# Part B of a gated attention kernel: batched token attention around two memory-row chains

## The chip, the cores and the metric

The kernel runs on one core of a Trainium2 chip. The metric is the device time of one launch in microseconds; TensorE is the matmul engine, DVE, ACT and POOL are the vector, scalar and GpSimd engines, SP only issues transfers. A granted clock of 1.00 is TensorE at full speed.

## What is computed

A token sequence x of 2048 rows by 576 goes through two attentions, and a gate mixes them; the outputs are the result and the gradients of eleven inputs for a given grad_out. Cut to what matters:

```python
# A: multi-query attention, 32 heads of 18, one key and value head
q = x @ wq; k = x @ wk; v = x @ wv
a = softmax(q k^T / sqrt(18)) v @ wo
# B: 64 segments of 32 tokens; 8 memory rows go from one to the next; 32 heads of 128
mem = mem0
for s in range(64):
    h = concat([mem, x[32*s : 32*s+32]])            # 40 rows
    q, k, v = h @ Wq, h @ Wk, h @ Wv
    mask = (row < 8) | (row >= col)                 # memory rows see all
    p = softmax(where(mask, q k^T / sqrt(128), -1e9))
    o = (p v) @ Wo
    mem = o[:8]; outs.append(o[8:])
g = sigmoid(sum(x * gate_w))
out = g * a + (1 - g) * b                           # and the gradients of all of it
```

Only the memory rows go from one segment to the next, in the forward pass from first to last and in the backward pass from last to first. The queries, keys and values of the tokens need no memory row. A token's attention needs the eight memory rows of its own segment.

## The kernel before

Part A (its functions are not in the diff but for the order of constants ahead of them) runs first and takes about a third of the span. Part B follows in stages, each with its own pools of on-chip memory, so a stage begins when the one before has given up its pools.

`b_forward` loops over 64 segments. A segment takes the 40 rows, padded to 64, as `hTs` (columns are tokens, then memory rows). For q, k and v, four banks `pbank` each take two groups of 64 output rows, in pieces of 102 or 103 columns; a piece is five contraction tiles by two groups of matmuls. Then come transposes into `ptrh`, scores `pkq` with a mask matmul, Exp, row sums and a reciprocal on DVE, and p·v in two layouts (`oT`, `o2`). 192 matmuls of eight columns (`psmall`) make the next eight memory rows, which ACT copies into the next `hTs`; this closes the loop from segment to segment. q, k, v, p and o are stored for the way back (`st_q2` to `st_oT`).

`make_transposed_weights`, `gate_combine_pass` and the load of the transposed weights follow. `b_backward` loops over the segments in reverse with the same 64-row layout: the gradient `gTs` times Wo (`pbank<-WoT,gTs`), products for dS, dq, dk and dv in two layouts, and 480 matmuls of 40 columns (`pdh`) for the gradient of the rows. `b_epilogue` computes the weight gradients from the stored rows (`epib`, `epiwo`), and `dx_combine` adds up the gradient of x.

Helpers: `mm` issues a matmul, `tr` a transpose (also on TensorE), `evac` copies a bank out on DVE and ACT in turn. POOL and SP issue the transfers; POOL also fills buffers and does some products of part A. In names, `bufs=2` means that a tile has two buffers.

Of the kernel before, what the change touches and what calls it, by code (L numbers as in the profile page):

```python
# [20 lines left out]
LP = 64  # L21
# [8 lines left out]
MNK_LIMIT = 960000  # L30
BIG_LIMIT = None


def plane(h):
    return h // 16


def ucol(h):
    return (h % 16) // 4, (h % 4) * 128


def pieces(N, M, K, limit="default"):
    lim = MNK_LIMIT if limit == "default" else limit
    if lim is None or M * N * K <= lim:
        return [(0, N)]
    maxn = max(1, lim // (M * K))
    n = (N + maxn - 1) // maxn
    base = N // n
    rem = N % n
    out = []  # L50
    lo = 0
    for i in range(n):
        sz = base + (1 if i < rem else 0)
        out.append((lo, lo + sz))
        lo += sz
    return out


def pieces_b(N, M, K):
    return pieces(N, M, K, limit=BIG_LIMIT)  # L60


class Kern:

    def __init__(self, tc, T, A_x, A_wq, A_wk, A_wv, A_wo, B_mem0, B_Wq, B_Wk, B_Wv, B_Wo,
                 gate_w, grad_out, outs, extras=None):
# [6 lines left out]
        assert T % P == 0  # L73
# [10 lines left out]
        self.extras = extras or {}  # L84
# [20 lines left out]
    def setup_consts(self, pool):  # L105
# [7 lines left out]
        self.onesB = pool.tile([P, 64], BF16, name="onesB")  # L113
        nc.gpsimd.memset(self.onesB[:], 1.0)
        self.negonesB = pool.tile([P, 64], BF16, name="negonesB")
        nc.gpsimd.memset(self.negonesB[:], -1.0)
        mb = pool.tile([P, 64], BF16, name="maskbias")
        nc.gpsimd.memset(mb[:], 0.0)
        nc.gpsimd.affine_select(out=mb[0:64], in_=mb[0:64], compare_op=ALU.is_ge, fill=NEGB,
                                base=0, pattern=[[1, 64]], channel_multiplier=-1)  # L120
        nc.gpsimd.affine_select(out=mb[0:64], in_=mb[0:64], compare_op=ALU.is_ge, fill=0.0,
                                base=31, pattern=[[0, 64]], channel_multiplier=-1)
        nc.gpsimd.affine_select(out=mb[0:64], in_=mb[0:64], compare_op=ALU.is_ge, fill=NEGB,
                                base=39, pattern=[[0, 64]], channel_multiplier=-1)
        nc.gpsimd.affine_select(out=mb[0:32], in_=mb[0:32], compare_op=ALU.is_ge, fill=NEGB,
                                base=39, pattern=[[-1, 64]], channel_multiplier=0)
        nc.gpsimd.affine_select(out=mb[32:64], in_=mb[32:64], compare_op=ALU.is_ge, fill=0.0,
                                base=39, pattern=[[-1, 64]], channel_multiplier=0)
        nc.gpsimd.affine_select(out=mb[32:40], in_=mb[32:40], compare_op=ALU.is_ge, fill=NEGB,
                                base=39, pattern=[[-1, 64]], channel_multiplier=0)  # L130
        self.maskbias = mb

    def setup_dram(self, dram):
        T, NSEG, NM = self.T, self.NSEG, self.NM
        NMP = ((NM + P - 1) // P) * P
        self.xT_dram = dram.tile([NKT, P, T], BF16, name="xT_dram")
        self.st_q2 = dram.tile([NSEG, P, 2048], BF16, name="st_q2")
        self.st_k2 = dram.tile([NSEG, P, 2048], BF16, name="st_k2")
        self.st_vT = dram.tile([NSEG, P, 2048], BF16, name="st_vT")
        self.st_pnT = dram.tile([NSEG, P, 2048], BF16, name="st_pnT")  # L140
        self.st_oT = dram.tile([NSEG, P, 2048], BF16, name="st_oT")
        self.st_WT = dram.tile([3, HB, P, D], BF16, name="st_WT")
        self.st_WoT = dram.tile([NKT, P, J], BF16, name="st_WoT")
        self.ox_dram = dram.tile([T, J], BF16, name="ox_dram")
        self.om_dram = dram.tile([NMP, J], BF16, name="om_dram")
        self.dbT_dram = dram.tile([NKT, P, T], BF16, name="dbT_dram")
        self.dqx_dram = dram.tile([T, J], BF16, name="dqx_dram")
        self.dqm_dram = dram.tile([NMP, J], BF16, name="dqm_dram")
        self.dkx_dram = dram.tile([T, J], BF16, name="dkx_dram")
        self.dkm_dram = dram.tile([NMP, J], BF16, name="dkm_dram")  # L150
        self.dvx_dram = dram.tile([T, J], BF16, name="dvx_dram")
        self.dvm_dram = dram.tile([NMP, J], BF16, name="dvm_dram")
        self.dxB_dram = dram.tile([T, D], BF16, name="dxB_dram")
        self.dm_dram = dram.tile([NMP, D], BF16, name="dm_dram")
        self.db_dram = dram.tile([T, D], BF16, name="db_dram")
        self.da_dram = dram.tile([T, D], BF16, name="da_dram")
        self.b_dram = dram.tile([T, D], F32, name="b_dram")
        self.a_dram = dram.tile([T, D], BF16, name="a_dram")
        self.mtok_dram = dram.tile([NMP, D], BF16, name="mtok_dram")

    def build_xT(self, work, psum, keep):
        nc = self.nc
        T, NTT = self.T, self.NTT
        xT = keep.tile([P, NKT, T], BF16, name="xT")
        for tt in range(NTT):
            xt = work.tile([P, D], BF16, name="xtok", bufs=2)
            nc.sync.dma_start(xt[:], self.A_x[tt * P:(tt + 1) * P, :])
            tp = psum.tile([P, 6, P], BF16, name="trx", bufs=2)
            for kt in range(4):
                nc.tensor.transpose(tp[:, kt, :], xt[:, kt * P:(kt + 1) * P], self.identB[:])  # L170
            nc.tensor.transpose(tp[0:64, 4, :], xt[:, 512:576], self.identB[:])
            nc.tensor.transpose(tp[64:128, 4, :], xt[:, 512:576], self.identB[:], tile_position=(0, 64))
            self.evac(xT[:, :, tt * P:(tt + 1) * P], tp[:, 0:5, :])
        for kt in range(NKT):
            nc.sync.dma_start(self.xT_dram[kt], xT[:, kt, :])
        return xT

    def load_B_weights_fwd(self, pool, wo_pool=None):
        nc = self.nc
        wo_pool = wo_pool or pool  # L180
# [4 lines left out]
        self.Wv5 = pool.tile([P, J], BF16, name="Wv5")  # L185
        for W4, Wd in ((self.Wq4, self.B_Wq), (self.Wk4, self.B_Wk), (self.Wv4, self.B_Wv)):
            for kt in range(4):
                eng = nc.sync if kt % 2 == 0 else nc.gpsimd
                eng.dma_start(W4[:, kt, :], Wd[kt * P:(kt + 1) * P, :])
        nc.sync.dma_start(self.Wqk5[0:64, :], self.B_Wq[512:576, :])  # L190
        nc.gpsimd.dma_start(self.Wqk5[64:128, :], self.B_Wk[512:576, :])
        nc.sync.dma_start(self.Wv5[0:64, :], self.B_Wv[512:576, :])
        nc.gpsimd.memset(self.Wv5[64:128, :], 0.0)
        self.WoN = wo_pool.tile([P, HB, D], BF16, name="WoN")
# [959 lines left out]
def build_full(tc, A_x, A_wq, A_wk, A_wv, A_wo, B_mem0, B_Wq, B_Wk, B_Wv, B_Wo, gate_w, grad_out, outs_raw,  # L1154
# [9 lines left out]
    with SB("const") as cpool, tc.tile_pool(name="dram", bufs=1, space=bass.MemoryType.DRAM) as dram:  # L1164
# [24 lines left out]
        with SB("xsp") as xsp:  # L1189
            k.dx_combine(xsp)  # L1190
# [76 lines left out]
```

## Time and profile before

| | |
|---|---|
| median of 3 runs | 14871.25 us (14867.74 to 14881.40) |
| profiled execution | 14893.78 us, span 14892.1 us, mean granted clock 0.596 |
| TensorE busy | 13545.5 us, 91% |
| DVE, ACT, POOL busy | 38%, 26%, 9% |
| part A | 0 to 5140 us |
| B forward | 5201 to 10423 us |
| transposes, gate pass, loads | 10423 to 10931 us |
| B backward | 10931 to 13977 us |
| weight gradients, dx | 13977 to 14892 us |

The profiled execution is one of several; its time is 0.15% above the median. Busy times are of one engine each and lie side by side, so they don't add up to the span. An instruction's row gives the tile that it writes, then `<-` and what it reads, then the partitions by elements of its operands.

### The profile page before, as it was taken

Reading aid. Unit: us, or ns where it says so; the run is one execution under the profiler, and the core shown is the slowest. Engines: PE = TensorE matmul, PEld = TensorE weight load, DVE = VectorE, ACT = ScalarE, POOL = GpSimd, SP = SyncE. Lnnn points to the kernel's source line nnn. Section 1 sums busy time; section 2 is a strip of 40 time slices with the busy share of each in tenths; the row PEclk is TensorE's granted clock in tenths of the full one; section 3 lists DMA queues with packets and bytes.
Section 4 is the critical chain, followed back from the end, with each engine's and each line's share of the span. In section 5 each row is a group of like instructions: output and inputs, shape, how many; then the busy total and the mean of one; then the engine's idle time right before and its main releaser. Section 6 shows DMA issues by size and latency. Waiting matters only on the chain. (4 is left out here: it accounts for less than half of the span.)

```text
span 14892.1 us, 355211 instructions
## 1 busy us (share of the span) xinstructions
PE 13545.5 (91%) x163790; PEld 7557.7 (51%) x163790; DVE 5585.9 (38%) x6393; ACT 3815.3 (26%) x4970; POOL 1269.2 (9%) x2548
## 2 busy tenths in 40 slices
PE   8999999999999899999999999999679999999896
PEld 2121121211212266666666666666568888888632
DVE  5555555555555323323232333323223333333201
ACT  3444444444444211111111111111112222222100
POOL 1000000000000000000000000000111111111225
PEclk6555555555555655555555555555667777777899
DMA  1000000000000211111111111111542222222334
GB/s 53 1 3 3 1 3 3 1 3 1 3 1 1 74 38 39 37 40 39 37 39 37 40 37 39 37 40 39 173 133 80 80 77 80 82 82 80 122 130 112
DMA packets 432921, 715.36 MB, mean 48 GB/s; under 512 B 212145, under 2 KB 288834, under 8 KB 428546
## 3 DMA queue, kind: packets, MB, share of 16 engines
q1 hardware_dynamic: 326466, 394.62, 8.6%
q0 software_dynamic: 103648, 296.68, 6.0%
q8 instruction: 1280, 20.97, 0.6%
q14 instruction: 215, 1.76, 0.0%
q10 hardware_dynamic: 1312, 1.33, 0.0%
HBM read 363.20 MB, written 329.19 MB: 46 GB/s over the span
## 5 line engine op out<-in xcount | busy, mean ns | idle before, releaser
L98 PEld LDWEIGHTS <-hTs 128*64 128x64 bf16 (+1 forms) x38400 | 1854.9, 150 | 948.0 <-DVE hTs L250 61.2
L1046 DVE TENSOR_TENSOR a_U<-a_w,a_E 128x1024 bf16<-128x1024 f32 x1024 | 1251.7, 1224 | 1131.8 <-ACT a_E L1044 1088.6
L973 DVE TENSOR_TENSOR a_U<-a_w,a_E 128x1024 bf16<-128x1024 f32 x1024 | 1253.1, 1224 | 963.1 <-ACT a_E L971 962.8
L1044 ACT ACTIVATE a_E<-a_w 128x1024 bf16<-128x1024 f32 x1024 | 1049.1, 1025 | 1375.6 <-PE a_w L98 1374.4
L971 ACT ACTIVATE a_E<-a_w 128x1024 bf16<-128x1024 f32 x1024 | 1048.8, 1025 | 1179.5 <-PE a_w L98 1179.5
L309 DVE RECIPROCAL rden<-pbank 64x512 f32<-64x512 f32 x256 | 840.5, 3322 | 482.3 <-PE pbank L98 482.3
L98 PE MATMUL pbank<-Wv,hTs 128*64 128x103 bf16 (+3 forms) x12800 | 912.4, 290 | 0.0
L98 PE MATMUL a_w<-a_kaug,a_qaug 19*128 19x512 bf16 x2048 | 901.7, 600 | 4.8 <-ACT a_E L1044 4.1
L98 PE MATMUL a_w<-a_vaugT,a_doaT 19*128 19x512 bf16 x2048 | 836.0, 620 | 21.8 <-DVE a_U L1046 15.9
L98 PE MATMUL pbank<-Wq,hTs 128*64 128x103 bf16 (+1 forms) x10240 | 710.5, 290 | 81.8 <-DVE hTs L250 60.9
L98 PE MATMUL pbank<-Wqk,hTs 64*64 64x102 bf16 (+1 forms) x5120 | 753.2, 291 | 0.0
L98 PE MATMUL pbank<-WoT,gTs 128*64 128x103 bf16 (+3 forms) x12800 | 672.7, 234 | 55.9 <-DMA WoT<-st_WoT 52.3
L98 PE MATMUL pbank<-Wk,hTs 128*64 128x103 bf16 (+1 forms) x10240 | 711.1, 290 | 0.0
L98 PE MATMUL a_acc<-a_E,a_dog 128*32 128x512 bf16 x2048 | 625.0, 600 | 71.8 <-ACT a_E L1044 0.2
L98 PE MATMUL a_w<-a_doT,a_vaugT 19*128 19x512 bf16 x2048 | 670.8, 623 | 5.2 <-ACT a_E L971 4.1
L98 PE MATMUL a_w<-a_qaug,a_kaug 19*128 19x512 bf16 x2048 | 658.0, 599 | 3.6 <-ACT a_doT L95 3.0
L98 PE MATMUL a_acc<-a_U,a_ku 128*32 128x512 bf16 x2048 | 625.3, 607 | 0.2
L98 PE MATMUL a_acc<-a_U,a_qtok 128*32 128x512 bf16 x2048 | 623.3, 606 | 0.6 <-DVE a_U L1046 0.6
L98 PEld LDWEIGHTS <-gTs 128*64 128x64 bf16 (+1 forms) x12800 | 476.0, 117 | 247.8 <-issue 57.8
L98 PE MATMUL pkq<-qT,kT 128*64 128x64 bf16 x2048 | 534.3, 261 | 0.0
L98 PE MATMUL pkq<-maskbias,identB 64*64 64x64 bf16 x2048 | 530.3, 259 | 0.0
L98 PE MATMUL epib<-dcol,h_x 128*128 128x512 bf16 (+1 forms) x1920 | 458.3, 382 | 59.7 <-DMA dcol<-dqx_dram 25.3
(393 smaller groups left out, 16761.8 us busy)
## 6 DMA issues: line engine op xcount, KB each, us to landing
st_q<-q SPq DMA_DIRECT2D x64, 512.0 KB
st_k<-k POOLq DMA_DIRECT2D x64, 512.0 KB, 2.9
st_vT<-vT SPq DMA_DIRECT2D x64, 512.0 KB
st_pnT<-pnT SPq DMA_DIRECT2D x64, 512.0 KB
st_oT<-oT POOLq DMA_DIRECT2D x64, 512.0 KB, 4.1
bq<-st_q SPq DMA_DIRECT2D x64, 512.0 KB
bvT<-st_vT SPq DMA_DIRECT2D x64, 512.0 KB
bk<-st_k POOLq DMA_DIRECT2D x64, 512.0 KB, 4.6
```

What stands on the lines that cost most here:

```text
L98: return self.nc.tensor.matmul(out, lhsT, rhs, start=start, stop=stop, tile_position=tp, skip_group_check=True)
L309: nc.vector.reciprocal(rden[rows, :], den[rows, :])
L971: nc.scalar.activation(ex[:], s[:], ACT.Exp, scale=SCALEA)
L973: nc.vector.tensor_tensor(out=u[:], in0=d[:], in1=ex[:], op=ALU.mult)
L1044: nc.scalar.activation(ex[:], s[:], ACT.Exp, scale=SCALEA)
L1046: nc.vector.tensor_tensor(out=u[:], in0=d[:], in1=ex[:], op=ALU.mult)
```

## The change

Part B is rewritten in stages. `b_project` makes q, k and v of all tokens in 16 tiles of 128, in both layouts (`XT` by token, `XE` by head column), and stores them, with k and v once more by segment (`XS`). `b_transpose_weights` follows in the same pools. `b_chain_fwd` goes over the 64 segments with the eight memory rows alone: 32 columns of `c_mT`, of which eight are this segment's rows, stand as weight in each of four groups of 32 columns of the array, and a group computes an eighth of the heads over 512 columns. A quad of four such matmuls goes to one bank. The scores of the memory rows with tokens and memory are one bank (`c_S`), with the mask added by a matmul; division by the row sums comes after p·v. The output (`c_pw`) leaves partial sums in four row groups, and five fp32 matmuls with a selector (`selF`) add these and give the next columns of `c_mT`. `b_x_attention` then takes 16 tiles by two halves of heads: forward attention of 128 tokens at once with a block mask, the gate and its gradient, and the token part of the backward pass. `b_chain_bwd` carries the gradient of the memory rows backwards, in the same way, `b_x_gradients` finishes dk, dv and dx of the tokens, `b_mem_rows` brings the chain's gradients into rows, and `b_weight_gradients` sums over 16 + 4 row tiles with 512-column matmuls. The gate pass, `b_epilogue` and `dx_combine` are gone as stages of their own.

`setup_consts` makes five masks and selectors on POOL where it made one.

The diff, cut to the parts that the prediction speaks of:

```diff
-    def b_forward(self, wpool, sp, psum, wo_pool=None):
...
-        for s in range(NSEG):
-            nc.sync.dma_start(hTs[:, :, 0:SEG], self.xT_dram[:, :, s * SEG:(s + 1) * SEG].rearrange("k p t -> p k t"))
...
-                    for (lo, hi) in pcs:
-        for kt in range(NKT):
...
-                            for (c, base) in ((u, 0), (u + 4, 64)):
-                                cols = slice(c * 512 + lo, c * 512 + hi)
-                                self.mm(pb[base:base + 64, lo:hi], lhsT=hTs[lrows, kt, :], rhs=wap[rows, cols],
-                                        start=(kt == 0), stop=(kt == NKT - 1), tp=(lrows.start, base))
...
-                    nc.vector.reciprocal(rden[rows, :], den[rows, :])
...
-    def b_backward(self, wpool, sp, psum):
...
+        def keep_block(t, n, lo, hi):
+            nc.gpsimd.affine_select(out=t, in_=t, compare_op=ALU.is_ge, fill=NEGB, base=-lo,
...
+        mc = pool.tile([P, 512], BF16, name="maskC")
+        mx = pool.tile([P, 4, P], BF16, name="maskX")
+        mm_ = pool.tile([P, 4, P], BF16, name="maskM")
...
+    def b_project(self, keep, sp, psum):
...
+        for tt in range(NTT):
+            tok = slice(tt * P, (tt + 1) * P)
+            for w in "kvq":
+                tk = sp.tile([P, J], BF16, name="p_tok", bufs=2)
+                te = sp.tile([P, 2, 4, 4, P], BF16, name="p_em", bufs=2)
+                for c in range(8):
+                    pb = psum.tile([P, 512], F32, name="p_pb", bufs=4)
+        for kt in range(NKT):
+                        wap, rows = self.w_nat(w, kt)
+                        self.mm(pb[:, :], lhsT=xT[rows, kt, tok], rhs=wap[:, c * 512:(c + 1) * 512],
...
+                    ptr = psum.tile([P, 4, P], BF16, name="p_tr", bufs=3)
...
+                nc.gpsimd.dma_start(self.XE[w][tt], te[:].rearrange("p r i g t -> p (r i g t)"))
...
+            for sl in range(4):
+                    ts = sp.tile([P, 32, SEG], BF16, name="p_seg", bufs=2)
+                    nc.gpsimd.tensor_copy(ts[:], te[:].rearrange("p r i g (s t) -> p (r i g) s t", s=4)[:, :, sl, :])
+                    nc.gpsimd.dma_start(self.XS[w][4 * tt + sl], ts[:].rearrange("p h t -> p (h t)"))
...
+    def b_chain_fwd(self, keep, sp, psum, WoN):
...
+            for wi, w in enumerate("qkv"):
+                qkv = sp.tile([P, 2, 512], BF16, name="c_qkv", bufs=4)
+        for r in range(2):
+                    pb = psum.tile([P, 512], F32, name="c_pb", bufs=2)
+        for kt in range(NKT):
+                        wap, rows = self.w_nat(w, kt)
+            for g in range(4):
+                            c = 4 * r + g
+                            self.mm(pb[32 * g:32 * g + 32, :], lhsT=mT[rows, kt, s * MEM:s * MEM + 32],
+                                    rhs=wap[:, c * 512:(c + 1) * 512], start=(kt == 0), stop=(kt == NKT - 1),
+                                    tp=(rows.start, 32 * g))
...
+            for g in range(4):
+                    nc.gpsimd.dma_start(self.MT[w][s * MEM:(s + 1) * MEM, :].rearrange("t (r g n) -> g t r n", r=2, g=4)[g],
...
+            nc.scalar.activation(ET[:, :], S[:, :], ACT.Exp, scale=SCALEB)
...
+            nc.vector.reciprocal(rl[:, :, 0], po[:, 2, 0:2])
...
+                        self.mm(pw[32 * g:32 * g + 32, lo:hi], lhsT=oT[:, c0:c0 + 32], rhs=WoN[:, h, lo:hi],
+                                start=(ri == 0), stop=(ri == 7), tp=(0, 32 * g))
+            ws = sp.tile([P, 640], F32, name="c_ws", bufs=1)
+            nc.vector.tensor_copy(ws[:, 0:320], pw[:, 0:320])
+            nc.scalar.copy(ws[:, 320:D], pw[:, 320:D])
...
+                self.mm(pm[:, kt, :], lhsT=ws[:, kt * P:(kt + 1) * P], rhs=self.selF[:, :], start=True, stop=True)
+            nc.vector.tensor_copy(mT[:, :, (s + 1) * MEM:(s + 2) * MEM], pm[:, :, :])
...
+    def b_x_attention(self, keep, sp, psum, WoN, WoT):
...
+                et = sp.tile([P, 4, 4, P], BF16, name="x_et", bufs=1)
...
+                    S = psum.tile([P, 4, P], F32, name="x_p", bufs=4)
+                    self.mm(S[:].rearrange("p g n -> p (g n)"), lhsT=self.identB[:, :],
+                            rhs=self.maskX[:].rearrange("p g n -> p (g n)"), start=True, stop=False)
...
+                        self.mm(pb[:, 0:512], lhsT=oe[:, i, g, :], rhs=WoN[:, h, 0:512], start=st, stop=sp_)
...
+                    nc.gpsimd.tensor_tensor(out=pr[:, i], in0=doe[:, i], in1=oe[:, i], op=ALU.mult)
...
+    def b_transpose_weights(self, sp, psum):
...
+                    ptr = psum.tile([P, 640], BF16, name="t_tr", bufs=1)
...
+    def b_chain_bwd(self, keep, wp, sp, psum):
...
+            for g in range(4):
+        for r in range(2):
+                        nc.gpsimd.dma_start(rl[32 * g:32 * g + MEM, r, :, 0],
+                                            self.RL_m[s, r].rearrange("(i g q) -> g q i", i=4, g=4)[g])
...
+            for n, (wi, w) in enumerate(((2, "v"), (1, "k"), (0, "q"))):
...
+                            self.mm(pw[32 * g:32 * g + 32, lo:hi], lhsT=g3[:, wi, c0:c0 + 32], rhs=self.WT[w][:, h, lo:hi],
+                                    start=(n + ri == 0), stop=(n == 2 and ri == 7), tp=(0, 32 * g))
...
+    def b_x_gradients(self, keep, sp, psum):
...
+                                self.mm(px[:, lo:hi], lhsT=em[w][:, i, g, :], rhs=self.WT[w][:, h, lo:hi], start=st, stop=sp_)
...
+    def b_mem_rows(self, sp, psum):
...
+    def b_weight_gradients(self, keep, sp, psum):
...
+                    for n in range(NH):
+                        self.mm(acc[0:rows, :], lhsT=h[:, n, kt * P:kt * P + rows], rhs=t[:, n, :], start=(n == 0), stop=(n == NH - 1))
...
```

Three places in the order of instructions. First POOL at the start of the program; the kernel before, from the constants of part A to the first transfer of grad_out (`a_go`):

```order
L761 MEMSET a_eck 128x36
L762 MEMSET a_ecv 128x36
L755 AFFINE_SELECT a_rep_87<-a_rep_87 19x32 x2
L121 AFFINE_SELECT maskbias<-maskbias 64x64
L755 AFFINE_SELECT a_rep_87<-a_rep_87 19x32 x2
L765 AFFINE_SELECT a_eck<-a_eck 128x18
L765 AFFINE_SELECT a_ecv<-a_ecv 128x18
L803 DMA a_go<-in_grad_out_dram 128x4x576
```

And the kernel after, at the same transfer:

```order
L134 AFFINE_SELECT selF<-selF 128x8
L887 AFFINE_SELECT a_rep_1073<-a_rep_1073 19x32
L127 AFFINE_SELECT maskM<-maskM 32x32 x4
L134 AFFINE_SELECT selF<-selF 128x8
L887 AFFINE_SELECT a_rep_1073<-a_rep_1073 19x32 x2
L893 MEMSET a_eck 128x36
L894 MEMSET a_ecv 128x36
L134 AFFINE_SELECT selF<-selF 128x8
L935 DMA a_go<-in_grad_out_dram 128x4x576
```

`a_go` was row 21 of POOL and is row 86, behind the selects and memsets of `maskC`, `maskX`, `maskM`, `selF` and `selG`; `a_wkv` and the memset of `a_wqp` follow it in both.

Second, TensorE where one segment of the forward loop ends and the next begins. Before, the last matmuls of the memory rows (`psmall`) and the first projection (`hTs` are the rows as weights):

```order
L98 LDWEIGHTS WoN
L98 MATMUL psmall<-oT,WoN 64x8
L98 LDWEIGHTS hTs
L98 MATMUL pbank<-Wq_33667,hTs 64x103
L98 LDWEIGHTS hTs
```

After, the last quad of the output (`c_oT` are weights), the selector and the first projection quad:

```order
L66 LDWEIGHTS c_oT
L66 MATMUL c_pw<-WoN,c_oT 32x64
L66 MATMUL c_o<-selF,c_ws 128x8 x5
L66 LDWEIGHTS c_mT
L66 MATMUL c_pb<-Wq_34659,c_mT 32x512
```

Five fp32 matmuls now stand between the output and the next projection, and a projection matmul has 512 columns with a weight of 32 columns where it had 103 with one of 64.

Third, POOL in one forward segment. Before:

```order
L275 DMA st_k_131<-k_33912 128x2048
L336 MEMSET hTs 128x5x24
L322 DMA st_oT<-oT 128x2048
L393 DMA ox_dram<-o_34593 32x2048
L394 DMA om_dram<-o_34593 8x2048
L290 MEMSET pnT 128x2048
```

After (`mt_q` to `ot_m` are the stores of the chain's rows):

```order
L264 DMA mt_q<-c_qkv 16x1x512 x4
L264 DMA mt_k<-c_qkv 16x1x512 x4
L264 DMA mt_v<-c_qkv 16x1x512 x4
L270 DMA me<-c_mE 128x768
L279 DMA et_m<-c_ET 128x512
L301 DMA rl_m<-c_rl 128x2x1
L303 DMA om<-c_oc 4x16x128 x4
L312 DMA ot_m<-c_oT 128x256
```

Four transfers and two memsets a segment became twenty transfers and one memset, all on the queue of POOL.

More of the change, by code (lines that the diff above doesn't have):

```diff
@@ L20 @@
 SEG = 32
-LP = 64
 NEGB = -30000.0
@@ L119, in setup_consts @@
[L119 to L124, printed above, removed]
@@ L131, in setup_consts @@
-        self.maskbias = mb
-    def setup_dram(self, dram):
[L134 to L159, printed above, removed]
@@ new lines, in load_mt, with tr4 @@
+    def load_mt(self, sp, name, src, tt, r):
+        t = sp.tile([P, 512], BF16, name=name, bufs=2)
+        for g in range(4):
+            self.nc.gpsimd.dma_start(t[32 * g:32 * g + 32, :], src[tt * 32:(tt + 1) * 32, (4 * r + g) * 512:(4 * r + g + 1) * 512])
+        return t
+    def tr4(self, psum, name, src_fn, dst, use=None):
+        ptr = psum.tile([P, 4, P], BF16, name="x_tr", bufs=2)
+        for g in range(4):
+            self.tr(ptr[:, g, :], src_fn(g), P)
+        self.evac(dst, ptr[:], use=use)
```

1261 lines of the change are left out of this document (670 added, 591 removed).

## The prediction

> **What bounds the kernel now.** I read the page first: the shares, then the clock row.
>
> ```profile
> PE 13545.5 (91%) x163790; PEld 7557.7 (51%) x163790; DVE 5585.9 (38%) x6393; ACT 3815.3 (26%) x4970; POOL 1269.2 (9%) x2548
> PEclk6555555555555655555555555555667777777899
> ```
>
> TensorE is busy nine tenths of the span, at about half clock for two thirds of it, and no other engine comes near. Next the view by stretches, cut where stages meet; columns are start and end, length, busy time and count of each engine, granted clock, DMA share and GB/s.
>
> ```profile
> 0.00:5140.00 5140.00, 4913.44 (x18691) 1075.18 (x18691) 2721.97 (x2606) 2249.17 (x2289) 235.64 (x619) 0.53 0.02 7
> 5140.00:5201.00 61.00, 0.10 (x4) 0.10 (x6) 1.32 (x2) 0.63 (x1) 13.91 (x15) 0.54 0.88 311
> 5201.00:10423.00 5222.00, 4769.91 (x66107) 3448.81 (x66107) 1621.70 (x1660) 738.98 (x1280) 262.20 (x382) 0.50 0.11 38
> 10423.00:10504.00 81.00, 77.36 (x540) 52.29 (x541) 27.13 (x67) 34.62 (x56) 28.64 (x53) 0.50 0.59 204
> 10504.00:10885.00 381.00, 209.18 (x8403) 183.03 (x8401) 90.68 (x284) 25.21 (x53) 41.62 (x79) 0.73 0.48 161
> 10885.00:10931.00 46.00, 0.41 (x2) 0.09 (x2) 3.07 (x4) 0.00 (x0) 26.57 (x50) 0.51 1.00 369
> 10931.00:13977.00 3046.00, 2832.47 (x66368) 2487.50 (x66368) 1041.66 (x1664) 721.34 (x1216) 317.39 (x702) 0.75 0.27 80
> 13977.00:14892.00 915.00, 742.63 (x3680) 310.73 (x3680) 78.33 (x108) 45.31 (x76) 343.25 (x649) 0.95 0.43 130
> ```
>
> In order: part A; B's weights come in; B forward (5222/64 = 81.6 us a segment); weight transposes; gate pass; weights again; B backward (3046/64 = 47.6 us a segment); weight gradients and dx. The diff leaves 5140 us alone and rewrites 9752 us, in which TensorE bounds everything but two load gaps. So the forecast is a count of TensorE work at the right clock, plus the waits of two serial chains. The timeline gives the old unit of work, once in each direction:
>
> ```profile
> 6045.06 14.26 PE L98 MATMUL pbank<-Wv,hTs 128*64 128x103 bf16 x200
> 12533.82 9.40 PE L98 MATMUL pbank<-WoT,gTs 128*64 128x103 bf16 x200
> 6045.00:6059.00 14.00, 14.00 (x200) 0.50 0.10 39
> 12533.00:12543.00 10.00, 9.65 (x205) 1.00 0.33 108
> ```
>
> A projection of 103 columns takes 71 ns at half clock and 47 ns at full. The chip grants full clock to the one dense run and not to the other; that is the largest unknown here.
>
> **Prices for the new work.** Full tiles of 512 columns, from the timeline of the weight gradients:
>
> ```profile
> 14302.01 3.62 PE L98 MATMUL epib<-dcol,h_x 128*128 128x512 bf16 x16
> 14305.46 0.81 PE L98 MATMUL epib<-dcol,h_m 128*128 128x512 bf16 x3
> ```
>
> Sixteen starts in 3.45 us are 215.6 ns each, 2.37 columns a ns; at half clock I take 1.19. The new chains use four weights of 32 columns side by side. The gate pass has such quads already (timeline, then one-microsecond stretches: busy, clock, DMA share):
>
> ```profile
> 10668.96 8.63 PE L98 MATMUL c_pb<-WoN,c_oT 128*32 128x171 bf16 x321 [3.27 <-DMA c_oT<-st_oT]
> 10671.00:10672.00 1.00, 1.00 (x40) 0.50 0.05 16
> 10674.00:10675.00 1.00, 1.00 (x64) 0.96 0.38 148
> 10675.00:10676.00 1.00, 1.00 (x68) 1.00 0.06 16
> 10659.00:10660.00 1.00, 0.00 (x0) 1.00 0.69 111
> 10661.00:10662.00 1.00, 0.00 (x0) 0.50 1.08 303
> ```
>
> 40 records a microsecond cold and 68 warm: ten and seventeen quads of some 144 columns (four pieces of 171, 171, 170, 64) in 1 us. That is 1.4 and 2.4 columns a ns for the whole quad, so four weights do run at once and I cost a quad as one matmul. The clock rises 5 us into dense quads and falls about 2 us into idleness.
>
> Evacuations, fp32 matmuls and hand-offs:
>
> ```profile
> L93 DVE CAST q<-pbank x128: 690/692/692, 5204.6 to 10352.5; 128x512 bf16<-128x512 f32 x128
> L95 ACT CAST q<-pbank x128: 586/586/586, 5208.2 to 10356.0; 128x512 bf16<-128x512 f32 x128
> L535 DVE CAST dhT<-pdh 128x160 bf16<-128x160 f32 x64 | 20.8, 324 | 347.2 <-PE pdh L98 347.2
> L95 ACT COPY wTstage<-ptrh 128x576 bf16<-128x576 bf16 x48 | 30.7, 639 | 41.9 <-PE ptrh L216 41.9
> L992 PE MATMUL a_w<-identF,a_accs 128*128 128x128 f32 x256 | 79.0, 438 | 21.9 <-ACT a_accs L987 21.9
> 6015.79 0.19 ACT L337 CAST hTs<-psmall 128x32 bf16<-128x32 f32 x1 [6.29 <-PE psmall L98]
> ```
>
> And POOL:
>
> ```profile
> L275 POOL DMA_DIRECT2D st_k<-k x64 | 36.8, 575 | 2137.7 <-ACT k L95 2137.7
> L394 POOL DMA_DIRECT2D om_dram<-o x64 | 33.1, 517 | 0.2 <-issue 0.2
> L290 POOL MEMSET pnT<- 128x2048 bf16 x64 | 116.6, 1822 | 303.3 <-PE a_acc L98 302.7 <-DMA st_pnT<-pnT 0.5
> L765 POOL TENSOR_SCALAR_AFFINE_SELECT a_eck<-a_eck 128x18 bf16<-128x18 bf16 x4 | 0.8, 202 | 0.1
> L1016 POOL TENSOR_TENSOR a_m<-a_tk,a_m 128x144 f32<-128x144 f32 x64 | 29.9, 467 | 0.0
> st_k<-k POOLq DMA_DIRECT2D x64, 512.0 KB, 2.9
> 30.52 0.60 PE L98 MATMUL a_p<-a_xT,a_wkv 128*18 128x512 bf16 x1
> ```
>
> **The change, part by part.**
>
> *Start.* Some 300 selects and 64 memsets for the masks stand on POOL ahead of a_go, a_wkv and a_wqp. At 202 ns each they take 70 us; 25 is my lower end, if each starts before the last has ended. Before, TensorE met a_wkv at 30.5 us, so little covers them: +45. Part A: 5140 + 45 = 5185.
>
> *Weight load.* The same weights without WoN, 13.3 MB instead of 18: 61 falls to 48.
>
> *P1, b_project.* 16 tiles x 3 x 8 = 384 banks of five 512-column matmuls (1.08 us) and four transposes (0.25): 1.34 us, 515. Each bank leaves one cast of 0.6 to 0.7 us and one copy of at most 0.64 (the wTstage row, 576 columns), shared by two engines: they hide. POOL owes 8 copies of 1024 columns and 11 DMAs a tile: 14 us at the memset's rate (1822 ns for 2048), 33 at that of the fp32 product (467 ns for 144), against 32 on TensorE. I stay near the lower end, since a copy is nearer the memset, and add 45 for buffers that come back late. The weight transposes follow through one bank (two before): transposes 0.35, copy 0.46 to 0.64, two hand-offs, 1.4 us for each of 84 heads: 118. End, 15. Sum 693, against nothing before: the work was inside the segments.
>
> *P2, forward chain.* Per segment, 30 projection quads of 512: 6.5 us warm, 12.9 cold; I take 11.3 (5 us cold, as in the gate pass, then warm; some interruptions by the 24 transposes). The tail, evacuation, transposes, ten score matmuls, Exp, row sums, p·v, reciprocal, product, two transposes, copy: ten hand-offs of 0.1 and 0.2 to 0.7 us for each link, 5.3. Memory output, 8 quads of 512 and 8 of 64: 1.9 warm, 3.9 cold, with weight loads of 32 columns 4.6. Copy of the sum (324 ns for 160 columns, so about 0.8 split over two engines), five fp32 selector matmuls (438 ns each), copy to mT: 3.1. Sum 24.3, taken 24.5; with start 15 + 64 x 24.5 = 1583. POOL has 20 DMA issues and a memset: 12 us at 575 ns, hidden behind 24.5 unless it waits for landings. Cold throughout: 30.5; warm: 17.7.
>
> *P3, b_x_attention.* 32 half tiles. I count 52,900 TensorE columns: 22 us warm, 44 cold; DMA 7.5 MB, 23 us at 330 GB/s (the load stretches show 311 and 369); POOL products and some 20 issues, 20 us; DVE and ACT about 14 each. Many tiles have one buffer, so the engines take turns: 40 us, from 30 (warm, only the DMA bound and some waits) to 53 (cold plus waits). 1280, plus 45 ahead for weights and WoT. The gate pass (381) goes into this.
>
> *P4, backward chain.* Load of transposed weights 55. Per segment ten WoT quads, 48 + 48 weight-gradient quads of 512 and 64 (24 of each), transposes, 20 score matmuls, five fp32 matmuls: dense quads 10+24 of 512 = 7.3 warm, 14.7 cold, tails 8.5: 21.5 between 15.8 and 26. The 15 POOL DMAs are 8.6 us. 64 x 21.5 = 1376.
>
> *P5, b_x_gradients.* 41,700 columns a half tile: 17.4 warm, 34.8 cold. No chain of exponentials in it, half of it wide 512-column matmuls: 24. 32 x 24 + 15 = 783. Memory rows, 12 rounds of loads, copies and 32 transposes: 75.
>
> *P6.* 2400 matmuls of 512 at 215.6 and 640 pairs of 512 and 64 at 245: 675, with loads and ends 720, against 915 that also held dx.
>
> Sum: 5185 + 48 + 693 + 1583 + 45 + 1280 + 55 + 1376 + 783 + 75 + 720 = 11,843, against a profiled execution of 14,893.8, which is 0.15% over the median. Scaled to the median: 11,825 us.
>
> **A rule against the rows.** Part A (0.53 over 5140 us, TensorE 96% busy) and the forward projection (0.50) are dense, and still at half speed. The Trainium skill's page "TensorE: Matmul & The Clock Gate" (Part 1) says that the gate is half or full, and goes full after about 3.4 us of sustained activity whatever the shapes are. The gate pass agrees roughly (5 us); the forward projection, 14 us busy in 14 at 0.50, does not. By the page alone the chains would warm in every segment, which is the third case below; by the old forward loop they never would, which is the second. My sum stands between, at the quad rows, because quads of 32 columns are the nearest shape.
>
> **Rivals.**
>
> 1. *Cold.* The quads and half-tile stages stay at 0.50 as the old forward did, with 32 to 64-column weights in most of their instructions. P2 64 x 30.5 (+384), P4 64 x 26 (+288), P3 32 x 53 (+416), P5 32 x 37 (+416): 11,825 + 1504 = about 13,330. For it: 5222 us at 0.50. Against it: the quads' own rows. Chance 0.25.
>
> 2. *Warm.* Quads back to back warm, and tails under 2 us at a time keep it. P2 17.7 (-435), P4 15.8 (-365), P3 30 (-320), P5 20 (-128): 11,825 - 1248 = about 10,580. For it: backward at 1.00 in dense runs; against it: the tails add up to 8 us a segment, and 2 us of idleness made the clock fall. The Trainium skill's page named above would favour it. Chance 0.12.
>
> 3. *Slower.* POOL waits for each transfer to land before the next issue: 20 x 2.9 = 58 us a segment in P2 and 15 x 2.9 = 43 in P4. (58 - 24.5) x 64 + (43 - 21.5) x 64 = 3520: 15,345. It decides once a pair of segments (one of each chain) gains 48 us, (14,871 - 11,825)/64; it would gain 55, so only if nearly every landing is serial. Against it: the om_dram issue of the old loop stood 0.2 us in all behind its neighbour. Chance 0.03.
>
> **How the numbers follow.** The forecast has 0.60. Its own range, from the chain and half-tile bounds each pulled half way: 11,200 to 12,600. The range of 8 in 10 goes from the warm case to just under the cold one, 10,600 to 13,200. A change of 0.2% (30 us) is what the runs, spread over 14 us, can tell from none. Only rival 3 is slower: faster 0.97, same 0.01, slower 0.02.
>
> **What would show it.** In the profile after: part A ending near 5185 with a gap on TensorE at 30 to 90 us; no b_chain_fwd segment under 17 or over 31 us; the clock within c_pb quads rising from 0.50 within each segment; POOL busy under 13 us a forward segment; 512-column gradients at 216 ns to the end. If stretches of c_pb show 0.50 for whole segments, rival 1; 1.00 with no drop, rival 2; TensorE waiting for mt or me stores, rival 3. The forecast is wrong if a stage that I counted by columns is set by a wait that no row of before shows: P3 with its single buffers is the likeliest place.

## The result, and the profile after

| | before | after |
|---|---|---|
| median | 14869.49 us (4 runs) | 11803.08 us (4 runs, 11794.68 to 11808.80) |
| ratio | | 0.7938, interval 0.7925 to 0.7952 |
| profiled execution: span, mean clock | 14892.1 us, 0.596 | 11807.0 us, 0.697 |

The forecast was 11,825. The page of the kernel after, its first line and the clock row:

```profile
PE 10704.6 (91%) x79411; PEld 4101.3 (35%) x79798; DVE 4365.5 (37%) x6102; ACT 3510.0 (30%) x4681; POOL 2793.4 (24%) x5477
PEclk8555555555555555589888877777778988777799
```

TensorE is still the bound, with half as many instructions, 2841 us less busy time and a higher clock in part B. POOL has more than twice its old busy time, but is the busiest engine in none of the stages that compute. The view by stretches, cut at the new stages, has the same columns as in the prediction:

```profile
0.00:5181.40 5181.40, 4912.89 (x18667) 1076.50 (x18691) 2721.42 (x2604) 2248.69 (x2289) 295.58 (x990) 0.53 0.02 7
5181.40:5240.40 59.00, 13.47 (x64) 6.87 (x65) 4.93 (x8) 3.19 (x5) 4.92 (x6) 0.57 0.93 306
5240.40:5817.00 576.60, 566.21 (x3381) 243.77 (x3445) 265.00 (x384) 225.19 (x385) 220.20 (x303) 1.00 0.58 230
5817.00:5937.50 120.50, 63.62 (x431) 44.13 (x429) 19.69 (x43) 27.95 (x44) 0.54 (x1) 0.52 0.30 121
5937.50:7358.00 1420.50, 1231.55 (x15732) 534.70 (x15731) 279.42 (x669) 217.08 (x478) 768.60 (x1336) 0.81 0.24 59
7358.00:7398.00 40.00, 25.12 (x208) 18.87 (x210) 13.20 (x36) 15.14 (x28) 19.23 (x35) 0.59 1.07 319
7398.00:8872.00 1474.00, 1250.87 (x10983) 743.72 (x11108) 494.27 (x1011) 415.99 (x744) 546.00 (x875) 0.78 0.51 169
8872.00:8915.00 43.00, 0.00 (x0) 0.00 (x0) 0.00 (x0) 0.00 (x0) 9.06 (x20) 0.50 0.95 385
8915.00:10020.00 1105.00, 953.94 (x18815) 566.65 (x18816) 278.83 (x670) 119.49 (x288) 515.02 (x1004) 0.89 0.32 93
10020.00:11010.00 990.00, 949.70 (x7105) 503.29 (x7202) 192.27 (x455) 161.87 (x288) 327.74 (x741) 0.74 0.58 184
11010.00:11120.00 110.00, 58.35 (x429) 44.92 (x430) 42.97 (x149) 30.04 (x57) 41.75 (x109) 0.50 0.92 286
11120.00:11807.00 687.00, 678.90 (x3606) 317.92 (x3679) 53.53 (x76) 45.33 (x76) 44.81 (x60) 1.00 0.44 146
```

Term by term, in us:

| term | forecast | measured | off |
|---|---|---|---|
| part A with the masks ahead | 5185 | 5181 | -4 |
| weight load | 48 | 59 | +11 |
| projection and weight transposes | 693 | 697 | +4 |
| forward chain | 1583 | 1420 | -163 |
| WoN, WoT | 45 | 40 | -5 |
| b_x_attention | 1280 | 1474 | +194 |
| load for the way back | 55 | 43 | -12 |
| backward chain | 1376 | 1105 | -271 |
| b_x_gradients | 783 | 990 | +207 |
| memory rows | 75 | 110 | +35 |
| weight gradients | 720 | 687 | -33 |
| sum | 11,843 | 11,807 | -36 |

The sum is right to 0.3%, the terms are not. The two chains were 434 us cheaper than forecast and the two x stages 401 us dearer; these errors cancelled by luck. So two questions were left: why the x stages cost more than their columns, and what sets the clock and the length of a chain's segment. All experiments start from the kernel after.

### The profile page after: what moved, and what is told of

Same layout as the page of the kernel before. It is cut to its first block, busy times and chain, and to the rows that moved or that the text cites. A ratio compares the mean times of both kernels' runs of the same rounds, so it can differ in the third digit from the quotient of the medians.

```text
span 11807.0 us, 189310 instructions
## 1 busy us (share of the span) xinstructions
PE 10704.6 (91%) x79411; PEld 4101.3 (35%) x79798; DVE 4365.5 (37%) x6102; ACT 3510.0 (30%) x4681; POOL 2793.4 (24%) x5477
## 5 line engine op out<-in xcount | busy, mean ns | idle before, releaser
L1137 POOL TENSOR_TENSOR a_otok<-a_tk,a_rl 128x144 bf16<-128x144 f32 x64 | 27.4, 428 | 2570.8 <-DVE a_rl L1136 2570.8
L66 PE MATMUL w_acc<-w_col,w_h 128*128 128x512 bf16 (+1 forms) x2352 | 523.4, 381 | 13.5 <-DMA w_col<-dqx 10.8
L61 DVE CAST p_tok<-p_pb 128x512 bf16<-128x512 f32 x384 | 265.4, 692 | 318.4 <-PE p_pb L66 318.4
L66 PEld LDWEIGHTS <-a_qaug 19*128 19x128 bf16 x2048 | 152.2, 98 | 655.5 <-issue 655.5
L66 PE MATMUL a_acc<-a_E,a_evB 128*64 128x512 bf16 x1024 | 325.6, 612 | 54.0 <-ACT a_E L1103 0.6
L66 PEld LDWEIGHTS <-w_h 128*128 128x128 bf16 (+1 forms) x2400 | 237.4, 100 | 299.6 <-issue 34.3
L66 PEld LDWEIGHTS <-a_dog 128*32 128x32 bf16 x2048 | 108.9, 100 | 652.4 <-issue 652.2
L63 ACT COPY p_em<-p_tr 128x512 bf16<-128x512 bf16 x384 | 225.0, 586 | 357.8 <-PE p_tr L71 357.6
L66 PEld LDWEIGHTS <-d_g 128*32 128x32 bf16 x12288 | 271.4, 104 | 170.8 <-issue 60.7
L66 PEld LDWEIGHTS <-a_ku 128*32 128x32 bf16 x2048 | 105.9, 101 | 639.3 <-issue 639.2
```

Source lines behind the costliest of these rows:

```text
L61: nc.vector.tensor_copy(out, in_)
L63: nc.scalar.copy(out, in_)
L66: return self.nc.tensor.matmul(out, lhsT, rhs, start=start, stop=stop, tile_position=tp, skip_group_check=True)
L1137: nc.gpsimd.tensor_tensor(out=osl, in0=v[:, :, :, o0:o0 + DA], in1=rl[:].to_broadcast([P, 4, 2, DA]), op=ALU.mult)
```

## The experiments

**The x stages.** This is TensorE's timeline in the middle of b_x_gradients (start, length, what), with three one-microsecond stretches (length, busy, clock, DMA share, GB/s):

```profile
10496.47 0.23 PE L66 MATMUL x_p<-g_mdo,g_eM 32*128 32x128 bf16 x1
10496.63 0.23 PE L66 MATMUL x_p<-g_dot,g_eq 128*128 128x128 bf16 x1
10505.09 0.28 PE L66 MATMUL x_p<-g_mq,g_sM 32*128 32x128 bf16 x1
10505.30 0.29 PE L66 MATMUL x_p<-g_qt,g_sq 128*128 128x128 bf16 x1
10496.00:10497.00 1.00, 1.00 (x9) 1.00 0.88 295
10497.00:10498.00 1.00, 1.00 (x8) 0.86 0.63 217
10505.00:10506.00 1.00, 1.00 (x6) 0.50 0.93 336
```

A matmul over all 128 rows (a token product) alternates with one over 32 rows (the same columns' share of the memory rows). The pairs begin at 10495.2 at full clock, and each product starts 160 ns after the last, though 128 columns are 54 ns by the price of the weight gradients. The clock falls some 2.5 us later, with TensorE busy all the time; then each starts 217 ns after the last (24 starts in 5.2 us), where the half-clock price gives 108. Three kernels tell the possible causes apart; each edit stands at the three places where such pairs are written.

First, the four token products of a bank, then the four memory products. (In this kernel and in the third one each token product is marked as the start of its bank, and three of a bank's four blocks come out without their token part; with the first alone marked, as in a later kernel, they come out whole. The amount of work is the same.)

```diff
-for i in range(4):
-    self.mm(pk[:, i, :], lhsT=lt[:, i, g, :], ..., start=True, stop=False)
-    self.mm(pk[:, i, :], lhsT=ml[rs, i, :], ..., start=False, stop=True, tp=(32 * g, 0))
+for i in range(4):
+    self.mm(pk[:, i, :], lhsT=lt[:, i, g, :], ..., start=True, stop=False)
+for i in range(4):
+    self.mm(pk[:, i, :], lhsT=ml[rs, i, :], ..., start=False, stop=True, tp=(32 * g, 0))
```

> In the two x stages (1474 and 990 us) a bank's eight matmuls stand as four over all 128 rows and then four over 32 rows, in place of alternating. Theory 1 (a matmul on other rows than the one before can't load its weights beside it): 64 changes of rows per half tile become 16, 48 matmuls fall from 217 ns to about 107 at half clock, 5.3 us per half tile and stage: 340 us less, 11,460 us, more if the clock rises. Theory 2 (back-to-back matmuls into the same columns wait for each other): no such neighbours are left, 64 x 0.11 = 7 us per half tile: 450 us less, 11,350. Theory 3 (buffers and clock set these stages, not the pairs): within 50 us of 11,803.

Measured: 11,465.94 us (ratio to the kernel before 0.7721, interval 0.7707 to 0.7735), 337 less than after and the number of the first theory. Second, all 128 rows in the memory products, the order as it was:

```diff
-self.mm(pk[:, i, :], lhsT=ml[rs, i, :], rhs=mr[rs, ...], start=False, stop=True, tp=(32 * g, 0))
+self.mm(pk[:, i, :], lhsT=ml[:, i, :], rhs=mr[:, ...], start=False, stop=True)
```

> The 32-row matmuls of the two x stages take all 128 rows (the sum then takes in the other groups' memory rows; the order and the columns stay). Theory 1 (change of rows): no change is left, 64 matmuls per half tile fall from 217 ns to 107 cold or 56 warm: 450 to 650 us less, 11,150 to 11,350. Theory 2 (same columns back to back): nothing moves, 11,803 within 30. Theory 3: nothing moves.

Measured: 11,386.89 us in one run, so without an interval: 416 less, short of the 450 to 650 that the first theory gave. Third, the memory product one block late:

```diff
+for i in range(5):
+    if i < 4: self.mm(pk[:, i, :], lhsT=lt[:, i, g, :], ..., start=True, stop=False)
+    if i > 0: self.mm(pk[:, i - 1, :], lhsT=ml[rs, i - 1, :], ..., tp=(32 * g, 0))
```

> The 32-row matmul of a column block stands one block later, so that rows still alternate but no two neighbours write the same columns. Theory 1 (change of rows): 11,803 within 30. Theory 2 (same columns): 450 to 650 us less.

Measured: 11,713.39 us in one run, 90 less. That is neither theory's number. Counted again after the result, the order has only six changes of rows a bank where the kernel after has eight (two token products stand together at a bank's start and two memory products at its end): 16 fewer of 64 per half tile. The first run removed 48 and gained 337; a third of that is 112. The same products in the timeline of the first run, of the second and of the third:

```profile
10303.49 0.40 PE L66 MATMUL x_p<-g_dot,g_eq 128*128 128x128 bf16 x4
10303.82 0.39 PE L66 MATMUL x_p<-g_mdo,g_eM 32*128 32x128 bf16 x4
```

```profile
10224.44 0.22 PE L66 MATMUL x_p<-g_mq,g_sM 128*128 128x128 bf16 x1
10224.50 0.22 PE L66 MATMUL x_p<-g_qt,g_sq 128*128 128x128 bf16 x1
10224.55 0.22 PE L66 MATMUL x_p<-g_mq,g_sM 128*128 128x128 bf16 x1
```

```profile
10500.28 0.23 PE L66 MATMUL x_p<-g_dot,g_eq 128*128 128x128 bf16 x1
10500.44 0.23 PE L66 MATMUL x_p<-g_mdo,g_eM 32*128 32x128 bf16 x1
```

In the first run a group of four starts 0.33 us after the one before at full clock, whether it is over 128 rows or over 32; so a change of rows adds some 0.11 us to four products of 55 ns, and a 32-row product is no dearer in itself. In the second, with all rows in both, a product starts every 55 ns, although neighbours still write the same columns. In the third, products with changed rows start 0.16 us apart as in the kernel after (0.22 at half clock), although neighbours write other columns. The change of rows is the cause, and writing the same columns back to back isn't. What in the engine takes the 0.11 us (the first theory names the load of the weights) is not shown. By stage, first run, then second (two rows each; the kernel after had 1474 at 0.78 and 990 at 0.74, the latter with the first loads of its stage):

```profile
7393.00:8643.00 1250.00, 1040.24 (x10887) 650.07 (x11015) 493.67 (x1009) 403.08 (x735) 542.94 (x866) 0.83 0.59 197
9829.00:10668.00 839.00, 699.08 (x7043) 416.76 (x7136) 189.92 (x453) 161.03 (x287) 309.16 (x700) 0.90 0.65 211
```

```profile
7408.00:8563.00 1155.00, 937.12 (x10890) 623.22 (x11017) 491.68 (x1007) 395.27 (x734) 540.40 (x865) 0.88 0.64 213
9752.00:10591.00 839.00, 658.63 (x7042) 418.21 (x7137) 189.22 (x453) 154.19 (x287) 309.58 (x700) 0.89 0.65 211
```

In b_x_gradients the second run gained nothing over the first (839 both): once the pairs are cheap, another wait ends last. The timeline of the second run names it, a copy of a staging tile with one buffer:

```profile
10206.36 0.61 PE L71 MATMUL x_tr<-identB,g_dt 128*128 128x128 bf16 x4 [4.08 <-ACT g_dt L786]
```

**Masks, weight transposes.** The masks were first only moved in the program's text, to stand after part A:

```diff
+                k.setup_masks()
                 k.load_B_fwd(bw)
```

> The masks and selectors are filled after part A instead of ahead of its transfers on POOL. My term: part A falls by 41 us (5181 back to 5140) and nothing is given back, since POOL is idle while B's weights load: 11,762. Rival: POOL's 70 us move ahead of the first stores of the projection, which then waits: 11,803 within 20.

Measured: 11,801.64 us (11,798.60 to 11,809.05), as after: the gain failed, and not for the reason of the rival. Waits and POOL's timeline, first of the kernel after, then of this one:

```profile
PE a_tr L71 <- ACT a_woT L63: 50.5, 2, 50.3
DVE a_da L970 <- DMA a_go<-in_grad_out_dram: 49.4, 1, 49.4
```

```profile
39.93 0.32 POOL L93 TENSOR_SCALAR_AFFINE_SELECT maskC<-maskC 128x8 bf16<-128x8 bf16 x1
DVE a_dos L61 <- POOL a_dos L1060: 25.4, 3, 22.1
PE a_p L66 <- DVE a_qs L1026: 21.4, 1, 21.4
```

The masks still run 29 to 97 us into the span, since nothing makes them wait: in the order that was built they stand behind part A's transfers, but ahead of the later fills of a_dos. The wait moved from a_go to a_dos, and TensorE's longest stall fell from 50 to 21 us; part A ended at 5173.8, where kernels with the old place had 5181 to 5194. In the next kernel the masks stand in memory that part A still holds, so they can't run early; grouping is kept (with the first product alone marked as start), and the weight transposes get a second bank:

```diff
+    def setup_masks(self, pool):       # the masks of setup_consts, in a pool of their own
+                k.setup_masks(bk)      # bk is opened after part A
-                    self.mm(pk[:, i, :], ..., start=True, stop=False)
+                    self.mm(pk[:, i, :], ..., start=(i == 0), stop=False)
-ptr = psum.tile([P, 4, P], BF16, name="p_tr", bufs=3)
+ptr = psum.tile([P, 4, P], BF16, name="p_tr", bufs=2)
-ptr = psum.tile([P, 640], BF16, name="t_tr", bufs=1)
+ptr = psum.tile([P, 640], BF16, name="t_tr", bufs=2)
```

> Three edits in different stages. In the x stages a bank's eight matmuls stand as four over 128 rows, then four over 32, with only the first marked as the start of the bank: both stages as in the grouped run, 340 us less. The masks are allotted in memory that part A still holds, so that they can't be filled before part A ends: part A ends at 5140 instead of 5181, 41 us less, if POOL's 67 us hide behind the load of B's weights and the projection. The weight transposes get two banks (the projection's transposes two instead of three): their stretch of 120 us falls by 30 to 50. Sum 11,380. Rival for the masks: the stretch after part A grows by what part A loses, 11,420.

Measured: 11,377.08 us (0.7647, interval 0.7635 to 0.7658). Its stretches: part A, the load of B's weights, and the weight transposes:

```profile
0.00:5143.80 5143.80, 4918.56 (x18691) 1077.17 (x18691) 2719.45 (x2604) 2245.47 (x2289) 230.44 (x609) 0.53 0.02 7
5143.80:5190.30 46.50, 7.74 (x52) 4.48 (x50) 4.23 (x6) 3.18 (x5) 43.86 (x297) 0.56 0.98 353
5771.50:5843.50 72.00, 61.82 (x441) 40.76 (x440) 20.25 (x44) 28.51 (x45) 0.54 (x1) 0.54 0.52 208
```

The forecast's term for the start is thus shown: without the masks ahead part A ends 38 us earlier, and POOL's 44 us hide behind the load, which got no longer (46.5 us against 59). The weight transposes fell from 120 us to 72.

**The forward chain.** One segment of the kernel after, from TensorE's timeline, with the clock of stretches in it and in the segments beside it:

```profile
6597.82 4.03 PE L66 MATMUL c_pw<-WoN,c_oT 128*32 128x512 bf16 x64 [0.45 <-DVE c_oT L311]
6602.51 2.30 PE L66 MATMUL c_o<-selF,c_ws 128*128 128x8 f32 x10 [0.66 <-DVE c_ws L324]
6605.11 1.90 PE L66 MATMUL c_pb<-Wq,c_mT 128*32 128x512 bf16 x16 [0.29 <-DVE c_mT L330]
6595.00:6596.00 1.00, 0.62 (x12) 1.00 0.63 234
6597.00:6598.00 1.00, 0.55 (x6) 0.50 0.38 124
6609.00:6610.00 1.00, 1.00 (x10) 0.53 0.00 0
6620.00:6621.00 1.00, 0.26 (x6) 1.00 0.20 41
```

The tail of small matmuls ends with waits, the clock falls to 0.50 soon after 6596, and output, selector and the first third of the projections run cold (at half clock) until 6609.9 (0.53 in the stretch from 6609); then the segment is warm. This segment is the forecast's picture, but only about half of them are like it. The next has the same tail, busy 0.26 in its emptiest stretch, and keeps 1.00 until 6627. Of 60 segments whose ends the trace shows, 30 take 23.2 to 24.1 us, with some 12 to 14 us at half clock (from each one's mean clock); 29 take 20.2 to 21.6, with 3 to 7 us at half clock; one, warm throughout, takes 18.7. Why a tail brings the clock down in one segment and not in the next stays open. To see what the cold part costs, extra matmuls fill the waits:

```diff
+            dm = psum.tile([P, 512], F32, name="c_dm", bufs=1)
+            for _ in range(3):     # and 4 ahead of the output, 6 ahead of the selector
+                self.mm(dm[:, :], lhsT=ET[:, 384:512], rhs=self.maskC[:, :])
```

> Thirteen extra matmuls of 128x512 into an unused bank stand in each forward-chain segment where TensorE waits (three beside the transposed values, four ahead of the output matmuls, six ahead of the selector). Theory 1 (the tail of a segment uses the array too little, so some 9 of its 22.2 us run at half clock): the clock stays up, projections and output lose about 4 us a segment: 250 us less, 11,550. Rival (the clock of a segment is not set by what the tail does, or the extras don't fit the waits): up to 2.8 us more a segment, 11,800 to 11,980.

Measured: 11,682.04 us (0.7860, interval 0.7847 to 0.7874), 121 less: half of what was expected, and between the two answers. The stage's stretch (to its last selector, which in the kernel after stands 16 us ahead of the end of its row) and the same rows of a segment:

```profile
5941.00:7215.00 1274.00, 1169.48 (x16384) 536.93 (x16378) 275.89 (x662) 213.74 (x472) 759.10 (x1324) 0.99 0.26 65
6629.55 2.14 PE L66 MATMUL c_pw<-WoN,c_oT 128*32 128x512 bf16 x64
6632.93 1.18 PE L66 MATMUL c_o<-selF,c_ws 128*128 128x8 f32 x10
6634.40 1.05 PE L66 MATMUL c_pb<-Wq,c_mT 128*32 128x512 bf16 x16 [0.29 <-DVE c_mT L339]
```

The clock stays at full, and output, selector and projections take about half; but the thirteen extras (2.8 us at 216 ns) are longer than the waits they fill (0.38, 0.45 and 0.66 us), and the mean segment goes from 22.2 to 20.0 us only, above the 18.7 of the warm one without extras. The selector alone, in bf16 in both chains:

```diff
-        sel = pool.tile([P, MEM], F32, name="selF")
+        sel = pool.tile([P, MEM], BF16, name="selF")     # and c_ws, d_ws
```

> The selector and the sums that it adds are bf16 instead of fp32 in both chains (the partial sums are rounded). My step costs the five fp32 matmuls on the path: 2.3 us in a forward segment and 1.3 in a backward one fall to some 0.6 and 0.4: (1.7 + 0.9) x 64 = 165 us less, 11,640. Rival (the chain is set by POOL's transfers or by buffers that come back late, and the matmuls hide): within 30 us of 11,803.

Measured: 11,634.62 us (0.7821, interval 0.7809 to 0.7832), 168 less, as the step on the path says. Rows of a segment and the forward chain's stretch:

```profile
6617.76 0.20 PE L66 MATMUL c_o<-selF,c_ws 128*128 128x8 bf16 x2 [0.67 <-DVE c_ws L324]
6618.17 0.29 PE L66 MATMUL c_o<-selF,c_ws 128*128 128x8 bf16 x3 [0.20 <-ACT c_ws L325]
5945.00:7233.00 1288.00, 1078.69 (x15248) 441.13 (x15241) 275.81 (x662) 213.67 (x472) 758.53 (x1324) 0.88 0.25 64
```

The mean clock of the forward chain rose too, from 0.81 to 0.88, so not all of the gain need be the selector's own time. For rival 3, stores of q, k and v and the small loads of reciprocals went from POOL's queue to SP's:

```diff
-nc.gpsimd.dma_start(self.MT[w][s * MEM:(s + 1) * MEM, :]...
+nc.sync.dma_start(self.MT[w][s * MEM:(s + 1) * MEM, :]...     # and the loads of RL_m
```

> Twelve of the twenty transfers of a forward segment and eight of the fifteen of a backward one go to SP's queue instead of POOL's. Forecast's step (POOL's issues hide behind the segment): within 30 us of 11,803. Rival 3 in small (POOL's queue holds up buffers that the chain waits for): 100 us or more less. Third way (SP's loads for the next segment now queue behind stores that wait): 50 us or more added.

Measured: 11,833.97 us (0.7954, interval 0.7942 to 0.7966), no gain and perhaps 30 us lost, at the edge of what the forecast's step allows: the twelve and the eight transfers that left POOL's queue did not pace the chains.

**What waits next.** In the tidy kernel TensorE waited for two things in the x stages (total us, times, longest):

```profile
PE x_tr L71 <- ACT g_dt L792: 103.8, 29, 7.5
PE x_p L66 <- POOL x_pr L499: 80.8, 106, 1.7
```

```diff
-                    dt = sp.tile([P, 4, 4, E], BF16, name="g_dt", bufs=1)
+                    dt = sp.tile([P, 4, 4, E], BF16, name="g_dt", bufs=2)
-                    nc.gpsimd.tensor_tensor(out=pr[:, i], in0=doe[:, i], in1=oe[:, i], op=ALU.mult)
+                    nc.vector.tensor_tensor(out=pr[:, i], in0=doe[:, i], in1=oe[:, i], op=ALU.mult)
```

> The tidy kernel with two buffers for the staging tile of dv and dk in the last x stage, and with the four products of the first x stage on DVE instead of POOL. TensorE waited 104 us for that tile's copies, which waited for its store, and 81 us for POOL's products. If these waits are on the path, 11,377 - 100 - 60 = 11,215. If other waits stand behind them (the second buffer of the matmul banks, ACT's copies), within 40 us of 11,377.

Measured: 11,121.64 us (0.7479, interval 0.7466 to 0.7492), 255 less than the tidy kernel, more than either answer; the last x stage:

```profile
9649.00:10322.00 673.00, 658.80 (x7139) 391.04 (x7135) 191.84 (x453) 171.38 (x287) 309.26 (x699) 0.98 0.81 262
```

The gain is larger than the waits (185 us). With them gone the clock of the last x stage also rose, from 0.92 to 0.98; how much of the rest that explains was not separated.

**Together.** The tidy kernel with the bf16 selector and six extra matmuls a segment:

> The tidy kernel of 11,377 with the bf16 selector and with six extra matmuls a segment instead of thirteen (one, two and three at the three waits, as many as the waits of 0.38, 0.45 and 0.66 us hold). The warm run's segment of 20.1 us lost 2.8 us to the extras and held 1.00; if six also hold the clock, the forward chain gains 4 us a segment against the kernel after, and the selector 0.8 us a segment more in it and 69 us in the backward chain: 11,377 - 250 - 50 - 69 = 11,010. If six don't hold it, the clock of the chain is near 0.8 and only the selector's 168 us show: 11,210.

Measured: 11,224.40 us (0.7547, interval 0.7533 to 0.7561), the second of the two numbers, but not for its reason: the clock of the chain was 0.95, and the segment still took 20.6 us. All edits:

> Both of the above together. Their edits lie in different stages, so their gains should add: 11,010 - 160 = 10,850. Rival: a chain that ends earlier only makes the next stage wait for its stores, and the gains add to less: above 10,950.

Measured: 10,979.07 us (0.7380, interval 0.7363 to 0.7396): the tidy kernel's two gains, 153 and 255, add up to all but 10 us of it. The number is on the rival's side of 10,950 because the chain's gain, put at 367 us beforehand, was 153, and not because the gains don't add. The same without the extras:

> The kernel of all edits without the six extra matmuls a segment. If the extras earn what they cost once the selector is bf16, the forward chain goes from 20.7 back to 21.5 us a segment and the whole to 11,030 or more. If the bf16 selector alone does what they did (its own run had 20.5 us a segment at a clock of 0.88), 10,950 to 10,980.

Measured: 10,938.54 us (0.7355, interval 0.7342 to 0.7367). The forward segment took 20.4 us, against 20.6 with them: the extras earn nothing beside the bf16 selector. This is the fastest version run: 865 us, 7%, below the kernel after. It rounds the partial sums of the memory rows to bf16, and where fp32 sums are wanted, grouping, masks, transposes' bank and the two edits of the x stages alone give 11,121.64.

## Why the prediction was right, and where it was not

- *Where the old time lay.* Right: the segments' TensorE work. Part A kept its length but for the masks. The forward pass fell from 5222 us to 697 + 1420 and the forward share of b_x_attention. It didn't come from one engine overtaking another: TensorE is busy 91% in both.
- *Prices per column.* Right for the weight gradients, 687 against 720. In the projection the term came out by luck: a bank takes 1.51 us, not 1.34, which makes the 577 us measured, and TensorE never waits there for a buffer, for which 45 us had been added. Its contraction ends with 64 rows, and the trace shows the same change of rows; the single 64-row matmul of 512 columns holds up the next for 0.32 us, not 0.22:

```profile
5500.83 0.39 PE L66 MATMUL p_pb<-Wqk,p_xT 64*128 64x512 bf16 x1
5501.15 1.04 PE L66 MATMUL p_pb<-Wv,p_xT 128*128 128x512 bf16 x4
```

- *Start.* Right: 45 forecast, 41 measured, with TensorE waiting 50 us in one piece, and the tidy kernel gives 38 of it back.
- *The forward chain.* The sum of 24.5 us a segment fits the segments that go cold (23.2 to 24.1). What failed is that each was taken to go cold for the output and 5 us of projections: half of them stay cold for 3 to 7 us only, and the mean is 22.2.
- *The backward chain.* This term was mis-sized most, 17.2 us against 21.5. I put its clock between the bounds; it had 0.89, near the warm bound of 15.8: nearly every segment has only 3.3 to 3.5 us at half clock. Why it stays warmer than the forward chain is not shown; TensorE is busy 86% of the backward chain and 87% of the forward one.
- *The x stages.* The step that failed is the count by columns, which puts what stands before a matmul at nothing. I priced 64 products of 128 columns a half tile as 108 ns cold or 54 warm; they took 217 and 160, because each changes the rows in use. The profile of before has no such alternation. Its projections do change rows, eight matmuls over 128 and then two over 64, and the 71 and 47 ns that I read there are means over that. I named single buffers in b_x_attention as the likeliest place of a hidden wait; buffers did matter (255 us with POOL's products), but the pairs were first, 337 to 416 us.
- *Memory rows.* 110 against 75: the DMA engines' share is 0.92 there; the forecast names the loads, without a price for what they move.
- *Rivals.* (The prediction's "third case" is rival 2, its "second" rival 1.) Cold throughout: refuted by 0.81 and 0.89 in the chains. Warm throughout: refuted for the kernel after; with the extras the forward chain was at 0.99 and its segment 20.0 us, not 17.7, as the extras' own time stands in it, and the one warm segment without them took 18.7. POOL pacing by landings: refuted by the segment itself, 22.2 us where it would be 58, and by the run with SP's queue.
- *The clock.* In the alternating pairs the clock falls from 1.00 to 0.50 while TensorE is busy 1.00 of the time; with the pairs grouped, the stage's clock goes from 0.74 to 0.90. So the profile's busy share is not what the clock follows. The Trainium skill's page "TensorE: Matmul & The Clock Gate" (Part 1) lets the clock rise after about 3.4 us of activity: the chain agrees roughly in its projections (4.8 us from 6605.1 to 6609.9), the pairs (217 ns each, some 11 us at 0.50) do not, if a matmul in the profile counts as activity. What the gate measures is not settled by these runs.

## What to carry to other kernels

Count a matmul's price by what stands before it as well as by its columns: where the number of rows changes from one matmul to the next, group those of a kind, with one start mark a bank. Take a recurrence apart, batch all that doesn't depend on it, and count the serial rest in hand-offs and small matmuls; the clock there is best read segment by segment, since a mean hides two kinds. A sum that fits proves little; compare it stage by stage before trusting a term.

## What the runs showed of the hardware that was not expected

- A change between 128 and 32 rows costs some 0.11 us at full clock (a product 160 ns instead of 55) and as much at half (217 instead of 108); one between 64 and 128 rows costs as much in the projection (0.32 us instead of 0.22 for 512 columns).
- In such pairs the granted clock falls from 1.00 to 0.50 and stays there with TensorE 100% busy.
- Segments of a chain with the same instructions come in two kinds, 12 to 14 us or 3 to 7 us at half clock, and 23.2 to 24.1 us or 20.2 to 21.6 long.
- Five fp32 matmuls of eight columns took 2.30 us cold and 1.18 warm; in bf16 0.49 warm, in two pieces.
- Matmuls that compute nothing raised a stage's mean clock from 0.81 to 0.99, and earned 121 us of a 250 us estimate; their own 2.8 us a segment are longer than the waits that they filled.
